# Cached grouped-query attention on one core: P·V two steps behind its scores, K three transfers ahead, last P·V by head group, held score weights

## The chip, the cores and the metric

One core of one Trainium2 chip runs the kernel. The metric is the device time of one execution in microseconds (us); lower is better. The profile is of one execution of the same program, taken by the hardware profiler.

## The reference

Each of 32 batches has 4 new tokens, 32 query heads and 4 key/value heads with a cache of 2048 positions. A query projection, attention over the whole cache, and an output projection are computed:

```python
B, Sq, D = 32, 4, 1024
Hq, Hkv, Sk, Dh = 32, 4, 2048, 128          # 8 query heads share a key/value head
q = (x @ wq).reshape(B, Sq, Hq, Dh).transpose(0, 2, 1, 3)
k = jnp.repeat(k_cache, 8, axis=1)
v = jnp.repeat(v_cache, 8, axis=1)
scores = einsum("bhqd,bhkd->bhqk", q, k) * Dh ** -0.5
o = einsum("bhqk,bhkd->bhqd", softmax(scores), v)
return o.transpose(0, 2, 1, 3).reshape(B, Sq, Hq * Dh) @ wo
```

All data are bfloat16. K and V of one batch are 2 MB each, so the caches alone are 128 MB; wq and wo are 8 MB each.

## The kernel before

Every operation is put into a list per engine by `p.op` or `p.dma`, in program order, with the names of the events that it waits for and the event that it sets. Each engine works its own list strictly in that order. An instruction that waits holds up everything behind it on its engine. "i" is the batch of a loop step and L = 31 the last batch.

**Loads.** All loads are issued by SP, in one list: x, the four parts of wq, then K and V by batch, one transfer of 2 MB each, and wo in four parts after V of batches 2 to 5. K and V have three buffers each (NKB = NVB = 3). `load_k(b)` (L133) waits until the last transposes of batch b−3 are done (`("fill", b-3, 7)`), `load_v(b)` (L142) until P·V of batch b−3 is done (`("pv", b-3)`). The order is K0, K1, then for each b: K(b+2), V(b). V of batch 31 is loaded in four pieces of 512 KB, one for each key/value head (L145). The twelve early output pieces follow on SP (L313).

**One loop step i** (the loop is near the end of the kernel) runs on TensorE in this order:

1. `pe_qk(i)` (L240): scores, 16 matmuls. Four column tiles of 32 hold 32 query rows (8 heads × 4 tokens) of one key/value head each; the loop goes over 4 chunks c of 512 positions and, inside, the 4 heads g. Each matmul has its own weight load. The result is in `ps_s` (128 × 2048 fp32[...]).
2. `pe_ot(i−2)` (L271): one transpose of the normalised o; ScalarE copies it to `oT_sb` (L275). After every eighth batch the output projection of that group of 8 batches follows (`oproj`, L296, 128 matmuls).
3. Two fills of batch i+1 (`pe_fill`, L207): K comes in natural layout, and TensorE transposes it, eight 128×128 blocks for each of eight fills. VectorE (L217) copies fills 2, 3, 5 and 7 to `KT_sb`, ScalarE (L219) the others.
4. The six other fills of batch i+1.
5. `pe_pv(i−1)` (L248): 64 matmuls (16 position blocks t × 4 heads g) with 32 columns of P^T as weights and V as moving operand.
6. `pe_pt(i, 0)`, `pe_pt(i, 1)` (L225): 16 transposes of P; VectorE copies each half to `PT_sb` (L231), which has one buffer, so the copy waits for P·V of batch i−1.

VectorE computes the row maximum (L280) and its scaled negative (L281), ScalarE the exponential with its row sum (L285), VectorE the reciprocal (L290). ScalarE normalises o after P·V (`o_evac`, L265). Fills, P^T, o, o^T and the projection's result rotate through a ring of four PSUM banks `ps_r`; a ring slot is free when the copy out of it is done.

**The end** is written out after the loop: o^T of batch 30, then P·V of batch 31 with heads 0 to 2 first and head 3 after them, two normalising copies on ScalarE (L357, L359), two transposes of o (L363, L371) with their copies (L364, L372), and the last output projection in two parts, heads 0 to 23 and 24 to 31 (L296 into `ps_s`). Then the last copy (L309) and four output transfers.

Of the kernel before, what the change touches and what calls it, by code (L numbers as in the profile page):

```python
# [5 lines left out]
ACT = mybir.ActivationFunctionType  # L6
ALU = mybir.AluOpType
AX = mybir.AxisListType
BF16 = mybir.dt.bfloat16
F32 = mybir.dt.float32  # L10


class _Program:
# [43 lines left out]
def bass_standalone__gqa_block_cached__sampling_kernel(  # L57
# [8 lines left out]
    B, Sq, D = x.shape  # L66
    _, G, Sk, Dh = k_cache.shape
    Hq = wq.shape[1] // Dh
    REP = Hq // G
# [6 lines left out]
    TV = T // C  # L76
    KT = D // 128
    NKB = 3
    NVB = 3
# [3 lines left out]
    OG = 8  # L83
    NOG = B // OG
    NC = D // 4
    scale = float(Dh) ** -0.5
# [5 lines left out]
    with ExitStack() as es:  # L92
        def sbuf(name, shape, dtype):
            return es.enter_context(nc.sbuf_tensor(name, shape, dtype))
# [6 lines left out]
        QT_sb = sbuf("QT_sb", [128, B, Hq, Sq], BF16)  # L101
        oT_sb = sbuf("oT_sb", [128, Hq, NT], BF16)
        P_sb = sbuf("P_sb", [128, Sk], BF16)
        PT_sb = sbuf("PT_sb", [128, TV, 128], BF16)
        x_sb = P_sb[:, 0:D]
        xT_sb = P_sb[:, D:2 * D].rearrange("p (a b) -> p a b", b=128)
        o_sb = sbuf("o_sb", [128, Dh], BF16)
# [15 lines left out]
        p = _Program()  # L123
# [8 lines left out]
        def load_k(b):  # L132
            p.dma("sp", lambda e: e.dma_start(  # L133
                K_sb[:, b % NKB, :, :], k_cache[b].rearrange("g (r t) d -> (g r) t d", r=R)),
                [("fill", b - NKB, NFILL - 1)] if b >= NKB else [], ("k", b), f"s_k{b % NKB}")
# [13 lines left out]
                wo_sb[:, 8 * c:8 * c + 8, :], wo[c * 1024:(c + 1) * 1024, :].rearrange("(h p) n -> p h n", p=128)),  # L149
                ["qproj"], ("wo", c), f"s_w{c}")  # L150

        load_k(0)
        load_k(1)
        for b in range(B):
            if b + 2 < B:
                load_k(b + 2)
            load_v(b)
            if b in (2, 3, 4, 5):
                load_wo(b - 2)
# [51 lines left out]
        def evac(b, f):  # L211
            buf = slot_of["kt", b, f]
            waits = [("fill", b, f)] + ([("qk", b - 1)] if b else [])
            dst = KT_sb[:, f * TB // C:(f + 1) * TB // C, :, :].rearrange("p v g (r c) -> p (v g) r c", c=C)
            src = buf.rearrange("p (c m r) -> p m r c", c=C, r=R)
            if f in DVE_FILLS:
                p.op("dve", lambda e: e.tensor_copy(dst, src), waits, ("kt", b, f))  # L217
            else:
                p.op("act", lambda e: e.activation(dst, src, ACT.Copy), waits, ("kt", b, f))  # L219

        def pe_pt(i, f):
            buf, waits = slot(("pt", i, f))
            buf = slot_of["pt", i, f] = buf.bitcast(BF16)
            for q in range(8):
                p.op("pe", lambda e, q=q: e.transpose(  # L225
                    buf[:, q * 128:(q + 1) * 128], P_sb[:, (8 * f + q) * 128:(8 * f + q + 1) * 128], ident[:, :]),
                    waits + [("exp", i)] if q == 0 else [], ("ptf", i, f) if q == 7 else None)

        def evac_pt(i, f):
            buf = slot_of["pt", i, f]  # L230
            p.op("dve", lambda e: e.tensor_copy(PT_sb[:, 8 * f:8 * f + 8, :].rearrange("p t q -> p (t q)"), buf),  # L231
                 [("ptf", i, f)] + ([("pv", i - 1)] if i else []), ("pt", i, f))


        def pe_qk(i):
            waits = [("kt", i, f) for f in range(NFILL)]
            waits += [("qe", j) for j in range(Hq // 4)] if i == 0 else [("exp", i - 1)]
            for c in range(4):
                for g in range(G):
                    p.op("pe", lambda e, c=c, g=g: e.matmul(  # L240
                        ps_s[32 * g:32 * (g + 1), c * 512:(c + 1) * 512],
                        lhsT=QT_sb[:, i, REP * g:REP * (g + 1), :],
                        rhs=KT_sb[:, 4 * c:4 * (c + 1), g, :],
                        start=True, stop=True, tile_position=(0, 32 * g)),
                        waits, ("qk", i) if (c, g) == (3, G - 1) else None)

        def pv_mm(buf, i, g, t, waits, done):
            p.op("pe", lambda e: e.matmul(  # L248
                buf[32 * g:32 * (g + 1), 0:Dh],
                lhsT=PT_sb[:, t, 32 * g:32 * (g + 1)],  # L250
                rhs=V_sb[:, i % NVB, g, t, :],
                start=(t == 0), stop=(t == TV - 1), tile_position=(0, 32 * g)), waits, done)
# [64 lines left out]
        for f in range(NFILL):  # L317
            pe_fill(0, f)
            evac(0, f)
        for i in range(B):  # L320
            pe_qk(i)
            softmax_max(i)
            if i >= 2:
                pe_ot(i - 2)
                ot_evac(i - 2)
                if i % OG == 1 and i > 1:
                    oproj(i // OG - 1)
            if i + 1 < B:
                for f in (0, 1):
                    pe_fill(i + 1, f)  # L330
                    evac(i + 1, f)
            softmax_exp(i)
            if i + 1 < B:
                for f in range(2, NFILL):
                    pe_fill(i + 1, f)
                    evac(i + 1, f)
            softmax_rinv(i)
            if i >= 1:
                pe_pv(i - 1)
                o_evac(i - 1)  # L340
            for f in range(2):
                pe_pt(i, f)
                evac_pt(i, f)


        L = B - 1
        pe_ot(L - 1)
        ot_evac(L - 1)
        o_l, waits = slot(None)
        waits = waits + [("pt", L, 0), ("pt", L, 1)]  # L350
        for t in range(TV):
            for g in range(3):
                pv_mm(o_l, L, g, t, waits + [("v", L, k) for k in range(3)] if t == 0 and g == 0 else [],
                      ("pva", L) if (t, g) == (TV - 1, 2) else None)
        for t in range(TV):
            pv_mm(o_l, L, 3, t, [("v", L, 3)] if t == 0 else [], ("pv", L) if t == TV - 1 else None)
        p.op("act", lambda e: e.activation(o_sb[0:96, :], o_l[0:96, 0:Dh], ACT.Copy, scale=rinv[0:96, L:L + 1]),  # L357
             [("pva", L), ("rinv", L), ("oT", L - 1)], "oa")
        p.op("act", lambda e: e.activation(o_sb[96:128, :], o_l[96:128, 0:Dh], ACT.Copy, scale=rinv[96:128, L:L + 1]),  # L359
             [("pv", L)], "ob")  # L360
        ta, waits = slot(None)
        ta = ta.bitcast(BF16)
        p.op("pe", lambda e: e.transpose(ta[:, 0:96], o_sb[0:96, :], ident[0:96, 0:96]), waits + ["oa"], "oTa")  # L363
        p.op("dve", lambda e: e.tensor_copy(  # L364
            oT_sb[:, 0:24, L * Sq:(L + 1) * Sq], ta[:, 0:96].rearrange("p (h s) -> p h s", s=Sq)), ["oTa"], "ota")
        y_l = ps_s[:, 0:512]
        n = NOG - 1
        oproj_mm(y_l, n, range(24), ["ota", ("ot", L - 1)], None)
        tb, waits = slot(None)
        tb = tb.bitcast(BF16)  # L370
        p.op("pe", lambda e: e.transpose(tb[:, 0:32], o_sb[96:128, :], ident[96:128, 96:128]), waits + ["ob"], "oTb")  # L371
        p.op("dve", lambda e: e.tensor_copy(  # L372
            oT_sb[:, 24:32, L * Sq:(L + 1) * Sq], tb[:, 0:32].rearrange("p (h s) -> p h s", s=Sq)), ["oTb"], "otb")
        oproj_mm(y_l, n, range(24, 32), ["otb"], ("op", n))
        oproj_evac(y_l, n)
        for m in range(NOG - 1):
            oproj_out(m, ("sp",))
# [57 lines left out]
```

## Time and profile before

| | before |
|---|---|
| device time, median of 9 runs | 387.11 us (385.98 to 387.68) |
| device time of the profiled execution | 387.25 us |
| its span on the core | 385.5 us |
| TensorE matmul busy | 281.7 us, 5929 matmuls |
| VectorE busy | 274.1 us |
| ScalarE busy | 208.4 us |
| moved by DMA | 152.32 MB, mean 395 GB/s over the span |
| mean granted TensorE clock | 0.946 |

The span is the time from the first to the last instruction on the core; 1.75 us of the profiled execution lie outside it. Busy time is the sum of the instructions of an engine; a share of it below 100% says nothing yet on what bounds the kernel. The chain of waits follows the work that ended last back through what released it. A DMA counts as landed when all its parts have landed.

### The profile page before, as it was taken

What the parts mean: (1) busy time and instruction counts of PE and PEld (TensorE: products, weight loads), DVE (VectorE), ACT (ScalarE), POOL (GpSimd) and SP (SyncE); (2) the same over time, 40 slices, a digit from 0 to 9 for tenths busy, and PEclk for the clock granted to TensorE, in tenths of its full rate; (3) what the DMA queues carried; (4) which work ended last, traced back from release to release, by engine and by line L of the source; (5) the groups of instructions that cost most, each with busy time, mean ns of one, the idle gap of its engine ahead of it and who ended that gap; (6) DMA issues with size and microseconds to landing.
All of it is one profiled execution on the core that took longest, in us unless ns stands there. A gap on an engine that the chain in (4) does not pass through costs nothing.

```text
span 385.5 us, 12595 instructions
## 1 busy us (share of the span) xinstructions
PE 281.7 (73%) x5929; PEld 230.8 (60%) x5929; DVE 274.1 (71%) x299; ACT 208.4 (54%) x261; POOL 0.7 (0%) x6
## 2 busy tenths in 40 slices
PE   2876888666383887887777778887759878876756
PEld 1875766556282766666655566665548666655545
DVE  0017999683553985998888849998868959997850
ACT  1005777355161646666666627766646566666620
POOL 0000000000000000000000000000000000000000
PEclk9999999896966999999999999999987999999978
DMA  8999999999999999999999999999999999999930
GB/s 328 432 432 414 420 418 396 414 407 399 411 408 414 415 420 412 417 415 419 417 416 419 417 413 420 416 414 417 413 417 416 420 416 418 419 417 409 375 140 9
DMA packets 27251, 152.32 MB, mean 395 GB/s; under 512 B 1472, under 2 KB 1984, under 8 KB 22592
## 3 DMA queue, kind: packets, MB, share of 16 engines
q1 hardware_dynamic: 27104, 151.49, 96.1%
q8 instruction: 46, 0.75, 0.8%
q10 hardware_dynamic: 96, 0.03, 0.0%
q14 instruction: 5, 0.04, 0.0%
HBM read 151.26 MB, written 0.26 MB: 393 GB/s over the span
## 4 chain that ended last, share of the span: by engine, by line
DMA 59%; PE 16%; ACT 12%; DVE 9%; issue 2%; SPq 1%
DMA K_sb<-in_k_cache_dram 59%; ACT KT_sb L219 6%; ACT P_sb L285 6%; DVE KT_sb L217 5%; PE ps_r L207 4%; PE ps_r L248 3%; DVE mx L280 3%; PE ps_r L296 3%; PE ps_r L225 3%; PE ps_s L240 2%; PE ps_s L296 1%; DVE PT_sb L231 0%; SPq L129 0%; ACT oT_sb L275 0%; DVE negmx L281 0%
## 5 line engine op out<-in xcount | busy, mean ns | idle before, releaser
L207 PE MATMUL ps_r<-ident,K_sb 128*128 128x128 bf16 x2048 | 143.3, 230 | 66.7 <-DMA K_sb<-in_k_cache_dram 41.5
L217 DVE COPY KT_sb<-ps_r 128x1024 bf16<-128x1024 bf16 x128 | 147.9, 1216 | 41.6 <-PE ps_r L207 41.5
L207 PEld LDWEIGHTS ps_r<-ident,K_sb 128*128 128x128 bf16 x2048 | 126.6, 104 | 82.3 <-DMA K_sb<-in_k_cache_dram 42.6
L219 ACT ACTIVATE KT_sb<-ps_r 128x1024 bf16<-128x1024 bf16 x128 | 124.4, 1026 | 72.1 <-PE ps_r L207 72.1
L280 DVE TENSOR_REDUCE mx<-ps_s 128x1 f32<-128x2048 f32 x32 | 73.3, 2292 | 6.7 <-PE ps_s L240 5.3
L285 ACT ACTIVATE P_sb<-ps_s,negmx 128x2048 bf16<-128x2048 f32 x32 | 63.0, 1970 | 2.2 <-DVE negmx L281 2.1
L231 DVE COPY PT_sb<-ps_r 128x1024 bf16<-128x1024 bf16 x64 | 41.4, 686 | 15.8 <-PE ps_r L225 14.2
L248 PE MATMUL ps_r<-V_sb,PT_sb 128*32 128x128 bf16 x2048 | 36.8, 223 | 16.6 <-ACT KT_sb L219 11.8
L248 PEld LDWEIGHTS ps_r<-V_sb,PT_sb 128*32 128x32 bf16 x2048 | 31.0, 98 | 22.1 <-ACT KT_sb L219 18.7
L275 ACT ACTIVATE oT_sb<-ps_r 128x128 bf16<-128x128 bf16 x31 | 8.6, 278 | 55.5 <-PE ps_r L271 55.5
L225 PE MATMUL ps_r<-ident,P_sb 128*128 128x128 bf16 x512 | 35.1, 223 | 1.7 <-ACT P_sb L285 1.3
L240 PE MATMUL ps_s<-KT_sb,QT_sb 128*32 128x512 bf16 x512 | 34.1, 382 | 2.3 <-DVE KT_sb L217 1.7
L225 PEld LDWEIGHTS ps_r<-ident,P_sb 128*128 128x128 bf16 x512 | 29.4, 99 | 5.3 <-ACT P_sb L285 1.5
L240 PEld LDWEIGHTS ps_s<-KT_sb,QT_sb 128*32 128x32 bf16 x512 | 10.8, 95 | 13.3 <-issue 2.8
L187 DVE CAST QT_sb<-ps_r 128x512 bf16<-128x512 f32 x2 | 1.3, 686 | 22.6 <-PE ps_r L176 22.6
L265 ACT ACTIVATE o_sb<-ps_r,rinv 128x128 bf16<-128x128 f32 x31 | 11.4, 367 | 9.8 <-PE ps_r L248 9.8
L189 ACT ACTIVATE QT_sb<-ps_r 128x512 bf16<-128x512 f32 x2 | 1.1, 594 | 26.1 <-PE ps_r L176 26.1
L176 PE MATMUL ps_s<-P_sb,w_sb 128*128 128x128 bf16 x128 | 9.7, 237 | 7.1 <-DMA w_sb<-in_wq_dram 7.1
L176 PEld LDWEIGHTS ps_s<-P_sb,w_sb 128*128 128x128 bf16 x128 | 8.6, 107 | 7.7 <-issue 4.4
L296 PE MATMUL ps_r<-w_sb,oT_sb 128*32 128x256 bf16 x384 | 11.3, 273 | 2.3 <-ACT oT_sb L275 1.2
L296 PEld LDWEIGHTS ps_r<-w_sb,oT_sb 128*32 128x32 bf16 x384 | 10.1, 97 | 3.2 <-issue 2.0
L271 PEld LDWEIGHTS ps_r<-ident,o_sb 128*128 128x128 bf16 x31 | 3.0, 98 | 12.7 <-issue 12.7
(30 smaller groups left out, 58.9 us busy)
## 6 DMA issues: line engine op xcount, KB each, us to landing
K_sb<-in_k_cache_dram SPq DMA_DIRECT2D x32, 2048.0 KB, 25.0
V_sb<-in_v_cache_dram SPq DMA_DIRECT2D x31, 2048.0 KB, 27.1
w_sb<-in_wq_dram SPq DMA_DIRECT2D x4, 2048.0 KB, 14.9
w_sb<-in_wo_dram SPq DMA_DIRECT2D x4, 2048.0 KB, 24.7
V_sb<-in_v_cache_dram SPq DMA_DIRECT2D x4, 512.0 KB, 15.5
P_sb<-in_x_dram SPq DMA_DIRECT2D x1, 256.0 KB, 2.7
out_dram<-y_sb SPq DMA_DIRECT2D x14, 16.0 KB, 11.5
out_dram<-y_sb ACTq DMA_DIRECT2D x2, 16.0 KB, 1.6
```

What stands on the lines that cost most here:

```text
L176: p.op("pe", lambda e, kt=kt, h=h: e.matmul(ps_q(h), lhsT=w_sb[:, kt, h * Dh:(h + 1) * Dh], rhs=xT_sb[:, kt, :], start=(kt == 0 and h % 4 ...
L207: p.op("pe", lambda e, q=q, t=t: e.transpose(buf[:, q * 128:(q + 1) * 128], K_sb[:, b % NKB, t, :], ident[:, :]), waits + [("k", b), "iden ...
L217: p.op("dve", lambda e: e.tensor_copy(dst, src), waits, ("kt", b, f))
L219: p.op("act", lambda e: e.activation(dst, src, ACT.Copy), waits, ("kt", b, f))
L225: p.op("pe", lambda e, q=q: e.transpose(buf[:, q * 128:(q + 1) * 128], P_sb[:, (8 * f + q) * 128:(8 * f + q + 1) * 128], ident[:, :]), wai ...
L231: p.op("dve", lambda e: e.tensor_copy(PT_sb[:, 8 * f:8 * f + 8, :].rearrange("p t q -> p (t q)"), buf), [("ptf", i, f)] + ([("pv", i - 1)] ...
L240: p.op("pe", lambda e, c=c, g=g: e.matmul(ps_s[32 * g:32 * (g + 1), c * 512:(c + 1) * 512], lhsT=QT_sb[:, i, REP * g:REP * (g + 1), :], rh ...
L248: p.op("pe", lambda e: e.matmul(buf[32 * g:32 * (g + 1), 0:Dh], lhsT=PT_sb[:, t, 32 * g:32 * (g + 1)], rhs=V_sb[:, i % NVB, g, t, :], star ...
L265: p.op("act", lambda e: e.activation(o_sb[:, :], buf[:, 0:Dh], ACT.Copy, scale=rinv[:, i:i + 1]), [("pv", i), ("rinv", i)] + ([("oT", i - ...
L280: p.op("dve", lambda e: e.tensor_reduce(mx[:, i:i + 1], ps_s[:, :], AX.X, ALU.max), [("qk", i)], ("mx", i))
L285: p.op("act", lambda e: e.activation(P_sb[:, :], ps_s[:, :], ACT.Exp, bias=negmx[:, i:i + 1], scale=scale, accum_out=ssum[:, i:i + 1]), [( ...
L296: p.op("pe", lambda e, h=h, j=j: e.matmul(buf[32 * j:32 * (j + 1), 0:NC], lhsT=oT_sb[:, h, 32 * n:32 * (n + 1)], rhs=wo_sb[:, h, NC * j:NC ...
```

## The change

It has five parts.

1. **P·V two steps behind.** Step i runs P·V of batch i−2 (was i−1) and o^T of batch i−3 (was i−2); the output projection of a group of 8 batches comes one step later. P·V of batch 30, o^T of 29 and of 30 move behind the loop.
2. **Load order.** K0, K1, K2, then for each b: K(b+3), V(b). Buffers and waits of each load stay as they were.
3. **Two P^T buffers.** `PT_sb` has two; a copy into it waits for P·V of batch i−2.
4. **The last P·V gives o^T.** P of batch 31 is normalised in place by one VectorE instruction over 128 × 2048 before its transposes. `pv_last(g)` has V (128 × 128) as weights and 32 columns of P^T as moving operand: 16 matmuls for each head group, after its own piece of V. One VectorE copy of 128 × 32 brings its o^T to `oT_sb`; `oproj_last(g)` does 32 matmuls of the output projection. TensorE's order is pv 0, pv 1, proj 0, pv 2, proj 1, pv 3, proj 2, proj 3. The ScalarE copies and TensorE transposes of the old end go.
5. **Held score weights.** Of the 16 score matmuls of a batch only those of the first chunk (c = 0) load weights; the 12 others are issued without a weight load and use what their column tile holds.

```diff
+def _matmul_held(nc, eng, out, lhsT, rhs, tile_position, start, stop):
+    return eng.add_instruction(mybir.InstMatmult(
...
+        tile_size=(128, 32),
+        tile_position=tile_position,
+        ldweights=False,
...
-        PT_sb = sbuf("PT_sb", [128, TV, 128], BF16)
+        PT_sb = sbuf("PT_sb", [128, 2, TV, 128], BF16)
...
-        load_k(0)
-        load_k(1)
+        for b in range(NKB):
+            load_k(b)
         for b in range(B):
-            if b + 2 < B:
-                load_k(b + 2)
+            if b + NKB < B:
+                load_k(b + NKB)
             load_v(b)
...
-                 [("ptf", i, f)] + ([("pv", i - 1)] if i else []), ("pt", i, f))
+                 [("ptf", i, f)] + ([("pv", i - 2)] if i > 1 else []), ("pt", i, f))
...
+                    if c == 0:
+                        mm = lambda e, a=(out, lhsT, rhs), g=g: e.matmul(
+                            a[0], lhsT=a[1], rhs=a[2], start=True, stop=True, tile_position=(0, 32 * g))
+                    else:
+                        mm = lambda e, a=(out, lhsT, rhs), g=g: _matmul_held(
+                            nc, e, *a, tile_position=(0, 32 * g), start=True, stop=True)
...
-            if i >= 2:
-                pe_ot(i - 2)
-                ot_evac(i - 2)
-                if i % OG == 1 and i > 1:
+            if i >= 3:
+                pe_ot(i - 3)
+                ot_evac(i - 3)
+                if i > OG and i % OG == 2:
                     oproj(i // OG - 1)
...
-            if i >= 1:
-                pe_pv(i - 1)
-                o_evac(i - 1)
+            if i >= 2:
+                pe_pv(i - 2)
+                o_evac(i - 2)
+            if i == L:
+                p.op("dve", lambda e: e.tensor_scalar(P_sb[:, :], P_sb[:, :], rinv[:, L:L + 1], None, op0=ALU.mult),
+                     [("rinv", L)], ("pn", L))
             for f in range(2):
-                pe_pt(i, f)
+                pe_pt(i, f, ("pn", L) if i == L else ("exp", i))
                 evac_pt(i, f)
...
+        pe_ot(L - 2)
+        ot_evac(L - 2)
+        pe_pv(L - 1)
+        o_evac(L - 1)
...
+        def pv_last(g):
+            buf, waits = slot(None)
+            for t in range(TV):
+                p.op("pe", lambda e, t=t: e.matmul(
+                    buf[:, 0:32], lhsT=V_sb[:, L % NVB, g, t, :], rhs=PT_sb[:, L % 2, t, 32 * g:32 * (g + 1)],
+                    start=(t == 0), stop=(t == TV - 1)),
+                    waits + [("v", L, g), ("pt", L, 0), ("pt", L, 1)] if t == 0 else [],
+                    ("pvl", g) if t == TV - 1 else None)
+            p.op("dve", lambda e: e.tensor_copy(
+                oT_sb[:, 8 * g:8 * (g + 1), L * Sq:(L + 1) * Sq], buf[:, 0:32].rearrange("p (h s) -> p h s", s=Sq)),
+                [("pvl", g)], ("otl", g))
+
+        def oproj_last(g):
+            oproj_mm(y_l, n, range(8 * g, 8 * (g + 1)), [("otl", g), ("ot", L - 1), ("exp", L)],
+                     ("op", n) if g == G - 1 else None)
+
         pe_ot(L - 1)
         ot_evac(L - 1)
-        o_l, waits = slot(None)
...
+        pv_last(0)
+        for g in range(G):
+            if g + 1 < G:
+                pv_last(g + 1)
+            oproj_last(g)
         oproj_evac(y_l, n)
```

More of the change, by code (lines that the diff above doesn't have):

```diff
@@ L10 @@
 F32 = mybir.dt.float32
+def _matmul_held(nc, eng, out, lhsT, rhs, tile_position, start, stop):
+    return eng.add_instruction(mybir.InstMatmult(
+        name=nc.get_next_instruction_name(),
+        engine=eng.engine,
+        start_tensor_calc=start,
+        stop_tensor_calc=stop,
+        tile_size=(128, 32),
+        tile_position=tile_position,
+        ldweights=False,
+        ins=[eng.lower_ap(rhs), eng.lower_ap(lhsT, for_matmul_weights=True)],
+        outs=[eng.lower_ap(out)],
+    ))
 class _Program:
@@ L219, in evac, with pe_pt @@
                 p.op("act", lambda e: e.activation(dst, src, ACT.Copy), waits, ("kt", b, f))
-        def pe_pt(i, f):
+        def pe_pt(i, f, ready):
             buf, waits = slot(("pt", i, f))
@@ L226, in pe_pt @@
                     buf[:, q * 128:(q + 1) * 128], P_sb[:, (8 * f + q) * 128:(8 * f + q + 1) * 128], ident[:, :]),
-                    waits + [("exp", i)] if q == 0 else [], ("ptf", i, f) if q == 7 else None)
+                    waits + [ready] if q == 0 else [], ("ptf", i, f) if q == 7 else None)
         def evac_pt(i, f):
             buf = slot_of["pt", i, f]
-            p.op("dve", lambda e: e.tensor_copy(PT_sb[:, 8 * f:8 * f + 8, :].rearrange("p t q -> p (t q)"), buf),
-                 [("ptf", i, f)] + ([("pv", i - 1)] if i else []), ("pt", i, f))
+            p.op("dve", lambda e: e.tensor_copy(PT_sb[:, i % 2, 8 * f:8 * f + 8, :].rearrange("p t q -> p (t q)"), buf),
+                 [("ptf", i, f)] + ([("pv", i - 2)] if i > 1 else []), ("pt", i, f))
         def pe_qk(i):
@@ L239, in pe_qk @@
                 for g in range(G):
[L240 to L245, printed above, removed]
+                    out = ps_s[32 * g:32 * (g + 1), c * 512:(c + 1) * 512]
+                    lhsT = QT_sb[:, i, REP * g:REP * (g + 1), :]
+                    rhs = KT_sb[:, 4 * c:4 * (c + 1), g, :]
+                    if c == 0:
[4 more added lines that the diff above has]
+                            nc, e, *a, tile_position=(0, 32 * g), start=True, stop=True)
+                    p.op("pe", mm, waits, ("qk", i) if (c, g) == (3, G - 1) else None)
         def pv_mm(buf, i, g, t, waits, done):
@@ L249, in pv_mm @@
                 buf[32 * g:32 * (g + 1), 0:Dh],
-                lhsT=PT_sb[:, t, 32 * g:32 * (g + 1)],
+                lhsT=PT_sb[:, i % 2, t, 32 * g:32 * (g + 1)],
                 rhs=V_sb[:, i % NVB, g, t, :],
@@ L319, in bass_standalone__gqa_block_cached__sampling_kernel @@
             evac(0, f)
+        L = B - 1
         for i in range(B):
@@ L322, in bass_standalone__gqa_block_cached__sampling_kernel @@
             softmax_max(i)
-            if i >= 2:
-                pe_ot(i - 2)
-                ot_evac(i - 2)
-                if i % OG == 1 and i > 1:
+            if i >= 3:
+                pe_ot(i - 3)
+                ot_evac(i - 3)
+                if i > OG and i % OG == 2:
                     oproj(i // OG - 1)
-            if i + 1 < B:
+            if i < L:
                 for f in (0, 1):
@@ L332, in bass_standalone__gqa_block_cached__sampling_kernel @@
             softmax_exp(i)
-            if i + 1 < B:
+            if i < L:
                 for f in range(2, NFILL):
@@ L343, in bass_standalone__gqa_block_cached__sampling_kernel @@
                 evac_pt(i, f)
-        L = B - 1
+        pe_ot(L - 2)
+        ot_evac(L - 2)
+        pe_pv(L - 1)
+        o_evac(L - 1)
+        y_l = ps_s[:, 0:512]
+        n = NOG - 1
+        def pv_last(g):
[9 more added lines that the diff above has]
+                [("pvl", g)], ("otl", g))
@@ L347, in bass_standalone__gqa_block_cached__sampling_kernel @@
+        def oproj_last(g):
+            oproj_mm(y_l, n, range(8 * g, 8 * (g + 1)), [("otl", g), ("ot", L - 1), ("exp", L)],
+                     ("op", n) if g == G - 1 else None)
         pe_ot(L - 1)
         ot_evac(L - 1)
-        o_l, waits = slot(None)
[L350 to L371, printed above, removed]
@@ L372, in bass_standalone__gqa_block_cached__sampling_kernel @@
-        p.op("dve", lambda e: e.tensor_copy(
-            oT_sb[:, 24:32, L * Sq:(L + 1) * Sq], tb[:, 0:32].rearrange("p (h s) -> p h s", s=Sq)), ["oTb"], "otb")
-        oproj_mm(y_l, n, range(24, 32), ["otb"], ("op", n))
+        pv_last(0)
[3 more added lines that the diff above has]
+            oproj_last(g)
         oproj_evac(y_l, n)
```

## The prediction

> **What bounds the kernel now.** I read the page's slices first, then its queues, then stages of the last 25 us, and last the chain and the timeline there.
>
> ```profile
> DMA  8999999999999999999999999999999999999930
> q1 hardware_dynamic: 27104, 151.49, 96.1%
> q8 instruction: 46, 0.75, 0.8%
> ```
>
> Tenths of DMA busy time in 40 slices, then packets, MB and share of two queues. From the second slice to the 37th the DMA engines are full, and nearly all of it is SP's own loads. No engine in that stretch sets the time: a step costs 8.65 us where the compute runs ahead (o^T transposes at 54.27, 62.92 and 71.56 in the timeline), but 4 MB of K and V take 10.0 us (K transfers released their transposes at 348.60 and 358.58). The slack is 1.4 us a step. So only a later start, a hole in the queue, a step above 10 us or the end can move the time.
>
> ```profile
> 362.00:364.00 2.00, 0.92 (x14) 0.58 (x11) 2.00 (x3) 2.00 (x4) 0.00 (x0) 1.00 1.02 403
> 364.00:366.00 2.00, 1.90 (x80) 1.80 (x80) 1.06 (x3) 1.33 (x3) 0.00 (x0) 1.00 0.72 274
> 370.00:372.00 2.00, 0.52 (x13) 0.35 (x14) 0.16 (x1) 2.00 (x3) 0.00 (x0) 0.87 0.55 202
> 372.00:374.00 2.00, 1.82 (x17) 1.56 (x15) 0.94 (x2) 0.17 (x2) 0.00 (x0) 0.50 0.22 72
> 374.00:376.00 2.00, 1.50 (x48) 1.50 (x52) 0.45 (x1) 0.14 (x1) 0.00 (x0) 0.50 0.00 0
> ```
>
> Columns: stretch, its length, busy time of PE, PEld, DVE, ACT and POOL with counts, clock, DMA share, GB/s. Half of the DMA engines are done near 365, the last ones near 374. The last piece of V31 (issued at 358.1, 15.5 us to landing) lands at 373.6, the first (355.2, 14.6) at 369.8. After it come 12 us without loads. Below are links of the chain in order of time (start, us, what), then two lines of the timeline.
>
> ```profile
> 358.54 0.05 issue
> ...
> 367.20 2.30 DVE mx L280
> ...
> 369.72 2.07 ACT P_sb L285 x2
> ...
> 371.83 1.90 PE ps_r L225 x16
> ...
> 374.50 3.16 PE ps_r L248 x61
> ...
> 378.15 2.85 PE ps_s L296 x72
> ```
> ```profile
> 368.75 0.94 PE L248 MATMUL ps_r<-V_sb,PT_sb 128*32 128x128 bf16 x53 [1.43 <-DMA V_sb<-in_v_cache_dram]
> 382.50 0.42 DVE L309 CAST y_sb<-ps_s 128x256 bf16<-128x256 f32 x1 [1.17 <-PE ps_s L296]
> ```
>
> The chain starts at K31's landing (358.54): its transposes, scores, maximum, exponential, P^T, P·V and projection end at 382.92, and output and end take 2.6 us more. P·V of 31 begins at 374.50, just after V31 is complete: both paths meet there.
>
> [...] clock 0.50 from about 371.5, after a quiet stretch, though not a fully idle one.
>
> **The change, part by part.** DMA volume and work per step are the same.
>
> *Load order.* K31 now has V28 to V31 behind it, where it had V29 to V31: it lands one transfer of 5.0 us earlier, at 353.6. V28 takes its place (358.5), V29, V30 and V31 keep theirs, since the same bytes pass the same engines. The queue's depth in mid-run stays: before, SP passed K(i+4), V(i+2) after fills and P·V of step i; now K(i+4), V(i+1), each needed one step later. At the start V0 now stands behind K3, which waits for the fills of batch 0 (34.4). Until then 3.4 + 4.2 + 4.4 + 1.9 = 13.8 MB have moved (336, 424, 436 and 430 GB/s); x, wq and K0 to K2 are 14.9 MB, 2.6 us more. The first load, x, took 2.7 us from issue to landing: no hole, at most 0.3 us. At the end V31 waits for P·V of 28, which now runs after the fills of K31 and V28's landing, near 359.2 to 360.3 (355.2 before). Its four issues took 4.1 us, so the fast engines, through with V30 at about 359, idle some 3 to 4 us; the slow ones, which set the end, reach V31 only at 368.6. Cost 0; behind V31 on SP stand only the outputs of finished groups.
>
> *P·V delay, two P^T buffers.* 64 P·V matmuls, a copy and a transpose per step move, none is added. P·V(i−2) meets V where P·V(i−1) did: one transfer behind the K filled just before. The P^T copy's wait gets looser. All lies under the loads: 0.
>
> *Held weights.* 32 × 12 = 384 loads of 95 ns (L240) go, overlapped with matmuls of 382 ns; a block of scores still streams for 1.05 us, so 0. The q8 row fetches 16 KB packets, so at most two fewer; each delays one DMA engine by about 1 us: 0 to −1.7 us, I take 0.
>
> *The end*, in the profile's time. K31 at 353.6. Scores of 31 started 7.5 us after K31's landing and ended 8.6 after: 362.2. P·V 29 runs at 363.7 (V29) for 1.1. Maximum, scaling and exponential end 13.2 after the landing: 366.8. Reciprocal 0.15; the normalisation is not in the trace. Nearest rows: P^T copy 686 ns for 1024 (PSUM source), so 1.3 for 2048; the maximum's 2.3 is a ceiling.[...] P^T starts at 367.8.
>
> From here TensorE is the path, and its clock decides. From 362.4 to 367.8 it does only 1.1 us of work, as little as ahead of the 0.50 stretch before. So I expect half speed from about 367 until[...] 371.8 to 374.8; middle 373.4. At half speed: 16 transposes 1.9 (to 369.7), o^T 29 0.3, P·V 30 from 370.1, 2 × 1.08 to 372.25 (V30 is there at 368.6), its copy 0.4, o^T 30, and the first pv_last at 372.75.
>
> Then pv_last: 64 matmuls with 128-column weights. The row L225 has such weight loads at 0.90/16 = 56 ns with more moving columns: 0.9 per group.[...] I take 56[...]. Projection: 128 × 28.8 ns (3.68 us at L296) = 3.68. Sum 3.6 + 3.68 = 7.28; its copies (0.17, as L372, plus 0.3 of waits) lie under the next 0.9 block, and pieces of V31 are ahead of it. Half speed until 373.4 adds 0.33: 380.35; latency 0.2, last copy 0.44: 381.0 against 382.92, **−1.9 us**. Removed with the old end: copies L357 and L359, two transposes, and the split P·V's 3.16 at half speed; they are inside this comparison.
>
> The profiled execution would then be 387.25 − 1.9 = 385.35; it lies 0.14 above the median, so 387.11 − 1.9 = **385.2**.
>
> **Rivals.** Chances in brackets.
>
> 1. *Forecast: faster, end bound by TensorE at partly half clock* (0.50). Clock back at 371.8 gives −2.5, at 374.8 −1.2: 384.6 to 385.9; with pv_last at 40 ns another −1.0.
> 2. *Faster, clock full at the end[...]* (0.27). At full clock P^T takes 1.0, P·V 30 starts at 369.0, pv_last at 370.5; +7.28, +0.64: 378.45, −4.5, 382.6.[...] Against it: the gap from 362.4. The bound from V31 (373.64 + 0.5 + 1.84 + 0.64 = 376.6) is −6.3.
> 3. *The gain is given back* (0.11). Half clock until 378.3, as before: 5.55 us at half lose 2.78: 372.75 + 7.28 + 2.78 + 0.64 = 383.45, +0.5; with partial recovery about 0. Against it: pv and projection leave no gap of the kind that stood at 373.7 and 376.4.
> 4. *Slower: held weights break the overlap of the four column tiles* (0.07). Then 16 score matmuls of 512 columns run in turn: 16 × 213 ns (the 1.05 us block, less 0.2 of latency, is 4 such rounds) = 3.4, +2.35 per step against 1.4 of slack: +0.95 × 30 = +28 us, 415. It decides from a block above 2.5 us. For it: no row shows a matmul without its load. Against: tiles, positions and streaming stay.
> 5. *The late normalisation or the order of loads costs more than it saves* (0.05): VectorE at 2.3 rather than 0.7 with half clock to 376 adds 1.6 + 0.6: +0.3; with a start hole of 1 us, 388.4.
>
> If the held form reloaded weights anyway, nothing changes in time.
>
> **How the numbers follow.** A difference of 0.2%, 0.8 us, is what a measurement here can tell from none. Cases 1 and 2 are faster (0.77, plus 0.01 of 3); 3 is mostly the same (0.10); 4 and 5 slower (0.12). The likeliest is 385.2. The range 382.3 to 387.4 holds case 1, case 2 nearly to the end of its full-clock form, and case 3.
>
> **What would show it.** K31's transposes start near 353.6; SP issues V31 near 360; V31's last piece still near 373.6; TensorE busy without a gap from about 368; a normalisation of about 0.7 us; pv_last groups of 0.9 us; score blocks of 1.05 us with 4 weight loads; the last copy ending near 381. Wrong if the last loads land more than 1 us from 373.6, if score blocks grow, or if the clock stays full after 367.

## The result, and the profile after

The changed kernel took 383.11 us (median of 10 runs, 382.3 to 383.94), the kernel before 386.89 us (32 runs, 384.83 to 387.68). The ratio is 0.9907, with a 95% interval of 0.9893 to 0.9922: 3.6 us faster. Measured a second time it was 0.9905 (0.9886 to 0.9924). The forecast was 1.9 us. The direction and the mechanism were right; the size forecast was little more than half of what came.

The page of the kernel after, slices of DMA busy time and two queues:

```profile
DMA  8999999999999999999999999999999999999870
q1 hardware_dynamic: 27104, 151.49, 97.1%
q8 instruction: 45, 0.74, 0.8%
```

The loads are as full as before, now in a span of 382.0 us instead of 385.5. Two stages of the kernel after (columns as in the prediction):

```profile
370.00:372.00 2.00, 2.00 (x59) 1.80 (x61) 1.21 (x2) 0.28 (x1) 0.00 (x0) 0.50 0.56 210
374.00:376.00 2.00, 2.00 (x73) 1.70 (x72) 0.38 (x2) 0.00 (x0) 0.00 (x0) 1.00 0.03 9
```

The loads still end near 374 (the DMA records have V31's last piece at 373.9). What differs is TensorE: it works in every moment of both stages, where before it had 0.52 us of work between 370 and 372. K31 has landed a transfer earlier; its transposes, which began at 358.58 before, begin at 352.36:

```profile
352.36 2.41 PE L223 MATMUL ps_r<-ident,K_sb 128*128 128x128 bf16 x40 [1.24 <-DMA K_sb<-in_k_cache_dram]
```

The chain of waits of the kernel after, near the end (start, us, what):

```profile
358.49 1.84 PE ps_r L268 x64
...
363.16 2.30 DVE mx L300
...
365.68 2.07 ACT P_sb L305 x2
...
367.96 0.77 DVE P_sb L363
...
368.78 1.86 PE ps_r L241 x16
...
370.75 1.77 PE ps_r L268 x63
...
373.27 0.86 PE ps_r L380 x32
374.13 0.99 PE ps_s L316 x32
...
377.10 1.89 PE ps_s L316 x64
...
379.01 0.42 DVE y_sb L329
```

It starts at V28 now, not at K31: P·V of 28 at 358.49, then maximum, exponential, normalisation (L363), P^T, P·V of 30, the new P·V (L380) and the projection (L316), which end at 379.43 instead of 382.92. The 3.49 us between these two are the whole difference of the spans.

This profiled execution took 383.77 us. Another one of the same kernel (after_again, 382.44 us) differs from it at two places that matter below, the first P·V of this stage and the end:

```profile
358.51 1.08 PE L268 MATMUL ps_r<-V_sb,PT_sb 128*32 128x128 bf16 x64 [1.20 <-DMA V_sb<-in_v_cache_dram]
...
377.58 0.42 DVE L329 CAST y_sb<-ps_s 128x256 bf16<-128x256 f32 x1 [1.68 <-PE ps_s L316]
```

P·V of 28 starts at the same time but takes 1.08 us instead of 1.84, because the half clock lies elsewhere (365.1 to 371.9), and the end comes 1.43 us earlier. Single traces must be compared with this in mind; the ratios are over all executions.

### The profile page after: what moved, and what is told of

The parts are those of the page before. It is cut to its first block, busy times and chain, and to the rows that moved or that the text cites. A ratio compares the mean times of both kernels' runs of the same rounds, so it can differ in the third digit from the quotient of the medians.

```text
span 382.0 us, 12207 instructions
## 1 busy us (share of the span) xinstructions
PE 278.8 (73%) x5927; PEld 220.3 (58%) x5543; DVE 274.7 (72%) x302; ACT 207.4 (54%) x259; POOL 0.7 (0%) x6
## 4 chain that ended last, share of the span: by engine, by line
DMA 60%; PE 16%; ACT 11%; DVE 10%; issue 2%; SPq 1%
DMA K_sb<-in_k_cache_dram 53%; DMA V_sb<-in_v_cache_dram 7%; ACT KT_sb L235 6%; ACT P_sb L305 5%; DVE KT_sb L233 5%; PE ps_r L223 4%; DVE mx L300 4%; PE ps_r L316 3%; PE ps_r L268 3%; PE ps_r L241 3%; PE ps_s L16 1%; PE ps_s L316 1%; PE ps_s L260 1%; DVE PT_sb L247 1%; PE ps_r L380 0%
## 5 line engine op out<-in xcount | busy, mean ns | idle before, releaser
L223 PE MATMUL ps_r<-ident,K_sb 128*128 128x128 bf16 x2048 | 138.2, 225 | 61.8 <-DMA K_sb<-in_k_cache_dram 36.8
L223 PEld LDWEIGHTS ps_r<-ident,K_sb 128*128 128x128 bf16 x2048 | 120.9, 101 | 79.7 <-DMA K_sb<-in_k_cache_dram 37.9
L268 PE MATMUL ps_r<-V_sb,PT_sb 128*32 128x128 bf16 x1984 | 35.8, 228 | 17.6 <-ACT KT_sb L235 12.6
L268 PEld LDWEIGHTS ps_r<-V_sb,PT_sb 128*32 128x32 bf16 x1984 | 30.1, 101 | 22.9 <-ACT KT_sb L235 22.0
L241 PE MATMUL ps_r<-ident,P_sb 128*128 128x128 bf16 x512 | 36.6, 228 | 4.3 <-DVE P_sb L363 4.0
L241 PEld LDWEIGHTS ps_r<-ident,P_sb 128*128 128x128 bf16 x512 | 30.8, 102 | 8.0 <-DVE P_sb L363 4.2
L16 PE MATMUL ps_s<-KT_sb,QT_sb 128*32 128x512 bf16 x384 | 26.3, 379 | 0.0
L260 PE MATMUL ps_s<-KT_sb,QT_sb 128*32 128x512 bf16 x128 | 12.8, 389 | 2.8 <-DVE KT_sb L233 1.7
L316 PE MATMUL ps_r<-w_sb,oT_sb 128*32 128x256 bf16 x384 | 11.5, 273 | 3.1 <-issue 1.9
L316 PEld LDWEIGHTS ps_r<-w_sb,oT_sb 128*32 128x32 bf16 x384 | 10.1, 97 | 4.0 <-issue 2.9
```

Source lines behind the costliest of these rows:

```text
L16: return eng.add_instruction(mybir.InstMatmult(name=nc.get_next_instruction_name(), engine=eng.engine, start_tensor_calc=start, stop_tenso ...
L223: p.op("pe", lambda e, q=q, t=t: e.transpose(buf[:, q * 128:(q + 1) * 128], K_sb[:, b % NKB, t, :], ident[:, :]), waits + [("k", b), "iden ...
L241: p.op("pe", lambda e, q=q: e.transpose(buf[:, q * 128:(q + 1) * 128], P_sb[:, (8 * f + q) * 128:(8 * f + q + 1) * 128], ident[:, :]), wai ...
L260: mm = lambda e, a=(out, lhsT, rhs), g=g: e.matmul(a[0], lhsT=a[1], rhs=a[2], start=True, stop=True, tile_position=(0, 32 * g))
L268: p.op("pe", lambda e: e.matmul(buf[32 * g:32 * (g + 1), 0:Dh], lhsT=PT_sb[:, i % 2, t, 32 * g:32 * (g + 1)], rhs=V_sb[:, i % NVB, g, t, : ...
L316: p.op("pe", lambda e, h=h, j=j: e.matmul(buf[32 * j:32 * (j + 1), 0:NC], lhsT=oT_sb[:, h, 32 * n:32 * (n + 1)], rhs=wo_sb[:, h, NC * j:NC ...
```

## The experiments

Differences in microseconds are ratios to the kernel before, times 387. Every kernel ran beside the kernel before on the same chip. Theory A is the prediction's mechanism with one price corrected. Its rivals are B (the new end alone is the gain), C (the held weights give a part) and, later, D (late instructions decide).

### The price of the new P·V

```diff
-                    buf[:, 0:32], lhsT=V_sb[:, L % NVB, g, t, :], rhs=PT_sb[:, L % 2, t, 32 * g:32 * (g + 1)],
+                    buf[:, 0:128], lhsT=V_sb[:, L % NVB, g, t, :], rhs=PT_sb[:, L % 2, t, :],
...
```

> The changed kernel, but the 64 matmuls of pv_last stream all 128 columns of P^T instead of 32 (the other 96 result columns are not used). Theory A: TensorE sets the end without a gap from P·V of batch 30 on, and the forecast missed by the price of one pv_last matmul (29 ns in the profile after, 56 in the sum). Then 64 x (56 - 29) = 1.7 us come back: 384.8 us, 1.9 below before, and pv_last groups of 0.9 us. Rival: V31's landing or something else sets the end and the price is hidden: 383.1, as the changed kernel.

384.64 us, ratio 0.9945 (0.9930 to 0.9959): 1.5 us slower than the changed kernel, 2.1 faster than before. One group each of the timelines of the kernel after and of wide_pv:

```profile
375.05 0.57 PE L380 MATMUL ps_r<-PT_sb,V_sb 128*128 128x32 bf16 x16
```
```profile
374.00 1.07 PE L380 MATMUL ps_r<-PT_sb,V_sb 128*128 128x128 bf16 x16
```

Both have the same weights and the same waits. With the moving operand as wide as the one from which I took 56 ns, a group takes 1.07 us, and the gain is back near the forecast. With 32 columns it takes 0.57; the chain has 0.50 for a group, 31 ns a matmul. So the price was wrong and it lies on the path: theory A. The two profiled executions themselves took the same time (383.82 and 383.77 us), since that of wide_pv lacks the half clock ahead of the scores; but from the first pv_last to the end of the projection it needed 7.78 us (371.14 to 378.92) against 5.78 (373.18 to 378.96).

### Which parts carry the gain

Each of these five undoes one part or does one part alone.

*The old end with everything else changed.*

```diff
...
-        pv_last(0)
-        for g in range(G):
-            if g + 1 < G:
-                pv_last(g + 1)
-            oproj_last(g)
+        o_l, waits = slot(None)
+        waits = waits + [("pt", L, 0), ("pt", L, 1)]
+        for t in range(TV):
+            for g in range(3):
...
```

> The changed kernel with the end of before: o = P·V for batch 31 in two parts, normalising copies on ScalarE, transposes, projection in two parts; no normalisation of P. Load order, P·V delay, two P^T buffers and held weights stay. Theory A: the gain comes from K31 landing a transfer earlier, and the new end is worth little, since it pays for the normalisation of P and its 1.0 us: about +0.7 on the changed kernel, 383.8. Theory B: the shorter work after V31 is the gain: 386 or more.

385.74 us, ratio 0.9977 (0.9965 to 0.9988): 0.9 us of the gain is left. Neither theory's number came. Timeline of old_end:

```profile
372.77 3.16 PE L268 MATMUL ps_r<-V_sb,PT_sb 128*32 128x128 bf16 x64 [2.44 <-DMA V_sb<-in_v_cache_dram]
376.42 3.37 PE L316 MATMUL ps_s<-w_sb,oT_sb 128*32 128x256 bf16 x96 [0.30 <-DVE oT_sb L388]
```

P^T is ready at 368.3, so the earlier K31 has done its part. But the old end asks for three pieces of V31 at once and idles for 2.44 us; then its P·V and the first 1.2 us of its projection run in a half-clock stretch (370.8 to 377.6). I had expected only +0.7 us on the changed kernel; it is +2.7.

*The new end alone, on the kernel before.*

```diff
...
+            if i == B - 1:
+                p.op("dve", lambda e: e.tensor_scalar(P_sb[:, :], P_sb[:, :], rinv[:, B - 1:B], None, op0=ALU.mult),
+                     [("rinv", B - 1)], ("pn", B - 1))
...
+        pv_last(0)
+        for g in range(G):
+            if g + 1 < G:
+                pv_last(g + 1)
+            oproj_last(g)
```

> The kernel before with only the new end (normalised P, pv_last by head group, projection by head group); load order, P·V one step behind and all weight loads stay. K31 lands at 358.5 as before, so P^T is ready near 375.3, 0.9 later than before because of the normalisation; then 1.9 + 3.7 us of TensorE work, part of it at half clock, against 8.4 us of the old end. Theory A (the two parts need each other): about 0.5 us below before, 386.3, far from the whole gain. Theory B (the new end alone is the gain): 383.5.

387.68 us, ratio 1.0021 (1.0011 to 1.0031): 0.8 us slower than before. Theory B falls, and the 0.5 us of gain that theory A expected did not come either. Timeline of new_end_only:

```profile
376.38 1.02 PE L356 MATMUL ps_r<-PT_sb,V_sb 128*128 128x32 bf16 x32 [0.77 <-DVE PT_sb L231]
377.32 1.90 PE L296 MATMUL ps_s<-w_sb,oT_sb 128*32 128x256 bf16 x32
```

P^T is ready only at 376.2, when V31 is complete (374.4): there is no landing left to work under, the normalisation is added, and projection blocks run at half speed. In this execution the loads also landed 0.8 us later than in the profile before, K31 at 359.34 instead of 358.54. It is the slowest of its 22 (386.98 to 388.59), so what the landings have to do with the +0.8 of the medians is not shown.

*The load order of before, all else changed.*

```diff
-        for b in range(NKB):
-            load_k(b)
+        load_k(0)
+        load_k(1)
...
-            if b + NKB < B:
-                load_k(b + NKB)
+            if b + 2 < B:
+                load_k(b + 2)
```

> The changed kernel with the load order of before (K0, K1, then K(b+2), V(b)); all else stays changed. Theory A: K31 lands a transfer (5.0 us) later, its exponential ends at 371.8 as before, normalisation, P^T, P·V 30 and the new end follow: about 4 us above the changed kernel, 387.2, no better than before. Theory B (the new end is the gain, the order of loads is not): 383 to 384.

387.90 us, ratio 1.0028 (1.0014 to 1.0042): 4.7 us above the changed kernel, 0.7 more than expected. Timeline of k_two_ahead:

```profile
373.18 1.89 PE L241 MATMUL ps_r<-ident,P_sb 128*128 128x128 bf16 x16 [3.68 <-DVE P_sb L363]
```

P^T of 31 starts at 373.18, in the kernel after at 368.78 (at 367.22 in after_again): 4.4 to 6.0 us, around the one transfer of 5.0. This kernel and new_end_only differ only in P·V's delay, the P^T buffers and the held weights; their ratios, 1.0028 and 1.0021, do not differ beyond their intervals. Without the new load order these three gained nothing.

*The load order alone, on the kernel before.*

```diff
-        load_k(0)
-        load_k(1)
+        for b in range(NKB):
+            load_k(b)
...
-            if b + 2 < B:
-                load_k(b + 2)
+            if b + NKB < B:
+                load_k(b + NKB)
```

> The kernel before with only the load order changed (K three ahead of V); P·V stays one step behind, one P^T buffer, old end, all weight loads. Theory A: P·V of batch i-1 now waits for a V that lands 15 us after the K of batch i+1 instead of 5, and it stands on TensorE ahead of the scores of the next batch. So P·V 28 starts at V28's landing (358.5), the transposes of K31 only near 361.5 though K31 is there at 353.6, and the exponential of 31 ends near 374.5 instead of 371.8: slower, about 389.5. Rival: the load order alone gives the gain: 383.5.

391.52 us, ratio 1.0120 (1.0102 to 1.0138): 4.6 us slower than before, where 2.6 were expected. Timeline of order_only:

```profile
358.41 1.08 PE L248 MATMUL ps_r<-V_sb,PT_sb 128*32 128x128 bf16 x64 [2.60 <-DMA V_sb<-in_v_cache_dram]
...
362.78 2.64 PE L207 MATMUL ps_r<-ident,K_sb 128*128 128x128 bf16 x40
...
375.64 0.35 PE L248 MATMUL ps_r<-V_sb,PT_sb 128*32 128x128 bf16 x11 [3.02 <-issue]
...
376.25 1.31 PE L225 MATMUL ps_r<-ident,P_sb 128*128 128x128 bf16 x16 [0.27 <-ACT P_sb L285]
```

P·V of 28 waits for V28, and the transposes of K31 start at 362.78, though K31 had landed at 353.15. That is the mechanism named. Part of the other 2 us is half clock (359.9 to 363.3), which the expectation did not have: P^T of 29 and the scores of 30, behind P·V of 28, ran slower, the transposes of K31 began 1.3 us later than the 361.5 expected, and the exponential ended at 376.20 instead of 374.5. The profiled execution is also the fastest of the four (390.60 to 392.12); the rest was not traced. In P·V of 30 TensorE then waited 3.02 us for nothing visible, of which more below. It cost nothing here: that P·V was done at 375.99, and P^T of 31 waited for the exponential anyway (last line).

*Held weights undone.*

```diff
-                    if c == 0:
-                        mm = lambda e, a=(out, lhsT, rhs), g=g: e.matmul(
-                            a[0], lhsT=a[1], rhs=a[2], start=True, stop=True, tile_position=(0, 32 * g))
-                    else:
-                        mm = lambda e, a=(out, lhsT, rhs), g=g: _matmul_held(
-                            nc, e, *a, tile_position=(0, 32 * g), start=True, stop=True)
+                    mm = lambda e, a=(out, lhsT, rhs), g=g: e.matmul(
+                        a[0], lhsT=a[1], rhs=a[2], start=True, stop=True, tile_position=(0, 32 * g))
```

> The changed kernel with a weight load for each of the 16 score matmuls again (held weights undone). Theory A: the loads lie under 512-column matmuls and the score block stays at 1.05 us; only 384 more instructions are fetched: within 0.3 us of the changed kernel. Rival C: the held weights gave a part of the gain, through shorter score blocks or through fewer instruction packets on the DMA engines: 0.8 us or more above the changed kernel.

 

> The changed kernel once more, beside the other kernels of this call on the same chip: 0.9907 of before as first measured, about 383.2 us. It is the base of the next differences. No theory differs on it.

383.05 us beside 383.46 of the changed kernel, measured together; ratios 0.9904 (0.9887 to 0.9920) and 0.9905. The score block, in the timelines of no_held and of the kernel after:

```profile
361.04 1.05 PE L259 MATMUL ps_s<-KT_sb,QT_sb 128*32 128x512 bf16 x16
```
```profile
362.08 0.40 PE L260 MATMUL ps_s<-KT_sb,QT_sb 128*32 128x512 bf16 x4
362.30 0.82 PE L16 MATMUL ps_s<-KT_sb,QT_sb 128*32 128x512 bf16 x12
```

From 362.08 to 363.12 it is 1.04 us, with 4 loads or with 16. Rival C falls, as far as a difference of 0.8 us can be seen here, and so does the prediction's fourth rival: the four column tiles still overlap, since 16 matmuls of 379 to 389 ns each fit into 1.04 us.

### The clock at the end, and a second limit

With the price settled I asked whether the half-clock stretches of the end (358.6 to 362.0 and 368.84 to 372.25 in the kernel after) could be taken away, by idle work on TensorE in its gaps: 24 transposes of the identity ahead of P·V of 28, and 44 behind P·V of 29, ahead of the P^T transposes.

```diff
...
+            if i == L - 1:
+                keep_warm("a", 24)
...
             if i == L:
+                keep_warm("b", 44)
```

> The changed kernel plus 24 idle transposes of the identity on TensorE ahead of P·V 28 and 44 ahead of the P^T transposes of batch 31, into a ring slot that nobody reads, to keep the clock granted. Theory A (the end is TensorE work, a part of it at half clock): in the profile after, half speed cost 0.8 us on P·V 28, 0.8 on P^T 30 and, later, 0.8 on P^T 31 and 0.7 on P·V 30; without it about 2 us less, 381.2, with V31's last landing (373.9 + 3.0) as the new bound. Rival: the clock is not on the path, or the idle transposes stand in the way: 383.1 or more.

384.05 us, ratio 0.9928 (0.9911 to 0.9945): 0.9 us slower than the changed kernel. The clock was full from 356.6 to the end, P^T took 1.07 us, and still the end came later. Timeline of warm:

```profile
365.89 0.68 PE L268 MATMUL ps_r<-V_sb,PT_sb 128*32 128x128 bf16 x34 [1.35 <-issue]
...
369.48 1.07 PE L241 MATMUL ps_r<-ident,P_sb 128*128 128x128 bf16 x16 [0.34 <-DVE P_sb L374]
...
371.90 0.63 PE L268 MATMUL ps_r<-V_sb,PT_sb 128*32 128x128 bf16 x32 [0.74 <-issue]
...
377.10 0.72 PE L324 MATMUL ps_s<-w_sb,oT_sb 128*32 128x256 bf16 x18 [0.90 <-issue]
```

In the middle of a block TensorE stops three times for nothing visible, 3.0 us in all. The first stop was over before the normalised P came, so about 1.6 us of it lay on the path; and P^T began at 369.48, 0.7 us later than in the kernel after, since the fillers ahead of P·V of 28 had pushed the scores back to 362.77. The DMA records of the instruction queue (q8) have a packet of 16 KB that ends at 364.44, 370.60 and 375.49, which is 1.3 to 1.6 us ahead of each resumption. This holds for the long stops of the other traces too: in the kernel before, the stops that end at 148.65, 229.42 and 310.99 follow packets that end at 147.12, 228.02 and 309.51. In the 16 traces there are 58 waits of TensorE for "issue" above 0.6 us, and 57 of them end 1.2 to 1.6 us after a packet; the one of order_only above ends 2.25 us after. So I read "issue" inside a block as late instructions (theory D). So the fillers were made longer and fewer, 6 and 11 matmuls of 512 columns in the same two places (warm_long; shown against warm):

```diff
...
-                p.op("pe", lambda e, q=q: e.transpose(
-                    buf[:, (q % 8) * 128:(q % 8 + 1) * 128], ident[:, :], ident[:, :]),
+                p.op("pe", lambda e: e.matmul(
+                    buf[:, 0:512], lhsT=ident[:, :], rhs=wo_sb[:, 0, 0:512], start=True, stop=True),
...
```

> As warm, with the same TensorE time filled by 6 and 11 matmuls of 512 columns instead of 24 and 44 transposes of 128: 102 fewer instructions, counting weight loads. In warm the clock was full to the end and yet 3.0 us of waits for nothing the profile shows stood on TensorE (1.35 in P·V 29, 0.74 in P·V 30, 0.9 in the projection). Theory D: those are late instructions[...]; then the long form has under 1 us of such waits and comes to 382 or less. Rival: the added TensorE work itself is in the way; then as warm, 384.1.

382.45 us, ratio 0.9891 (0.9875 to 0.9906), and no stop above 0.6 us after 240. About the same busy time (4.0 against 4.1 us) with fewer instructions is 1.4 us faster than warm. Against the changed kernel it is 0.6 us, inside the intervals. In warm_few 6 of them stand ahead of P·V of 29 and 8 behind it, none ahead of P·V of 28; few_split also normalises P in two halves.

```diff
...
             if i == L:
+                keep_warm("b", 6)
             if i >= 2:
                 pe_pv(i - 2)
                 o_evac(i - 2)
             if i == L:
+                keep_warm("c", 8)
...
```
```diff
...
+                for f in range(2):
+                    half = P_sb[:, 1024 * f:1024 * (f + 1)]
+                    p.op("dve", lambda e, half=half: e.tensor_scalar(half, half, rinv[:, L:L + 1], None, op0=ALU.mult),
+                         [("rinv", L)], ("pn", f))
...
```

> The changed kernel plus 14 matmuls of 512 columns on TensorE, 6 ahead of P·V 29 and 8 behind it, where it waits for V29 and for the normalised P. Theory A (half clock at the end costs): P^T of 31 at 1.07 instead of 1.86 us and P·V 30 at 1.08 instead of 1.81, so 1 to 1.5 us below the changed kernel, about 382.0. Rival: the clock is worth nothing, because V30 and V31 land late enough to hide it: 383.2.

 

> As warm_few, with the normalisation of P in two halves, each followed by its own transposes. Half of 0.75 us comes off the path: 0.3 us below warm_few, about 381.7. If V30's landing (368.5) holds up P·V 30 anyway: as warm_few.

Both came out at 386.7 us, ratios 0.9997 (0.9978 to 1.0015) and 0.9989 (0.9966 to 1.0011): 3.3 to 3.6 us worse than the changed kernel, against both theories in their text. few_split's timeline shows how:

```profile
370.38 0.89 PE L392 MATMUL ps_r<-PT_sb,V_sb 128*128 128x32 bf16 x19
374.64 0.51 PE L392 MATMUL ps_r<-PT_sb,V_sb 128*128 128x32 bf16 x13 [3.37 <-issue]
```

TensorE stops after the third matmul of the second group. The packet that began at 368.15 in the kernel after and at 368.29 in the profile of warm_few began at 372.22 here, and half clock came with the stop (371.7 to 378.5). The lateness is not the same in every execution: of the 14 executions of warm_few the traced one took 382.32 us and has no such stop, while the other 13 took 386.07 to 387.91; one of few_split's 14 took 382.05. If late packets are the cause, moving the packet boundaries must move the time, and one must ask whether the measured change owes its size to such a boundary. So 24 idle transposes (48 instructions) were put near 4.6 us, where TensorE waits for wq:

```diff
+        for q in range(24):
+            p.op("pe", lambda e, q=q: e.transpose(
+                ring[3].bitcast(BF16)[:, (q % 8) * 128:(q % 8 + 1) * 128], ident[:, :], ident[:, :]))
```

> warm_few with the same 24 idle transposes near 4.6 us. The unprofiled runs of warm_few lay near 386.7, its profiled one at 382.3, and few_split's profile has a 3.4 us wait for nothing visible in pv_last, which ends 1.5 us after an instruction packet. Rival D (late instructions): the padding moves the boundary and the time changes by 2 us or more, to about 382.5. If the added 512-column matmuls themselves cost the 4 us: still 386.7.

 

> The changed kernel plus 24 idle transposes of the identity on TensorE near 4.6 us, while it waits for the first part of wq: 48 more instructions ahead of all others, 2.6 us of work under the wait. Theory A (the gain comes from K31's earlier landing and the new end): 383.2, as the changed kernel. Rival D (where the packets[...] begin decides whether TensorE runs dry at the end, and the changed kernel has a lucky place): up to 4 us more, 386 to 387.

 

> The kernel before with the same 24 idle transposes near 4.6 us. Theory A: 386.9, as before. Rival D: the place of the instruction packets costs the kernel before something that the padding changes: off by more than 1 us, to either side.

| kernel | without padding | with padding |
|---|---|---|
| before | 1 | 1.0001 (0.9987 to 1.0016) |
| changed | 0.9905 (0.9886 to 0.9924) | 0.9896 (0.9881 to 0.9910) |
| warm_few | 0.9997 (0.9978 to 1.0015) | 0.9903 (0.9886 to 0.9920) |

The padding takes 3.6 us away from warm_few and nothing from the two kernels compared here. So the 3.6 us of warm_few hang on where its instructions begin, and the change's gain does not hang on it, as far as this one shift shows. That the 3.6 us are a late packet is shown only for few_split, a near relative, by its trace; for warm_few it is inferred, since no execution near 386.7 us was traced. Why a packet comes late in some executions and not in others stays open. Full clock at the end, without the stops, was worth no more than the 0.6 us of warm_long here; few_pad, whose half-clock stretch only moved to an earlier place (359.4 to 362.8), is level with the changed kernel. No version is shown to be better than it.

## Why the prediction was right in kind and short in size

- **Loads set the pace and do not move.** Right. V31's last piece at 373.9 against 373.6; no hole at the start; SP issued V31 at 360.36, as forecast near 360, and it cost nothing.
- **K31 one transfer earlier.** Right: its transposes began at 352.36, 1.2 us ahead of the 353.6 of the sum. That was spent again: a half-clock stretch from 358.6 to 362.0, not forecast, stretched P·V of 28 and P^T of 30 to 1.8 us each, and the scores of 31 began at 362.08 against 361.1. In after_again, without that stretch, they began at 360.52.
- **Exponential and normalisation.** The exponential ended at 367.75 against 366.8; the normalisation took 0.75 us. The sum counts 0.7 for it, a number that the trace of before did not show; the nearest row there gave 1.3.
- **Half clock from about 367 until about 373.4.** Right in kind, and over P^T and P·V of 30 as forecast, but it came later and ended earlier: 368.84 to 372.25 (365.1 to 371.9 in after_again). Its end, 371.8 to 374.8 in the forecast, was my estimate: the trace of before did not show what ends such a stretch. First pv_last at 373.15 against 372.75. That this came out so close is partly luck: in after_again it was 371.70.
- **The step that failed: pv_last's price.** 64 × 56 ns = 3.6 us was the term; the chain has 0.86 + 0.50 + 0.50 = 1.86. These 1.7 us are all of the gap between 381.0 and 379.43 and more. The row that I took streams 128 columns, and its 56 ns were not a limit of its weight load: with such loads and 32 columns 27 to 31 ns were measured in the chain. The 1.5 us between wide_pv and the changed kernel are this term, turned on and off.
- **Old end against new end.** The sum compared two absolute ends and never priced the old end under the new load order. old_end shows that it would have lost 2.7 us; the load order and the delay without the new end bring 0.9, the new end without them −0.8, all together 3.6. The forecast was right to cost them as one path.
- **Nothing for held weights, P^T buffers, P·V's delay in mid-run.** For the held weights no_held shows it. P·V's delay and the two P^T buffers were not tried alone, but with the old load order the three together gained nothing (k_two_ahead beside new_end_only). With the new order they are worth 5.5 us: old_end (0.9977) and order_only (1.0120) differ in just these three. So the delay costs nothing and is what lets the new order gain.

## What to carry to other kernels

When loads bound a kernel, look at what stands between the landing of the last operand and the end: reorder the loads so that the long chain's operand comes first, move the work that waits for the other operand out of that chain's way, and cut the work on the last operand by its pieces. Here the new order alone lost 4.6 us, with P·V delayed it gained 0.9, the new end alone lost 0.8, and all together gained 3.6. Price a small matmul by its own moving width: 16 with the same weights took 0.57 us with 32 moving columns and 1.07 with 128, so here the wider row only bounded it from above. And a few microseconds at the end can be instructions that come late (3.37 us in few_split); more instructions near the end can make that worse (3.0 us of stops in warm), and a shift of where they begin can take it away (3.6 us, few_pad against warm_few).

## What the runs showed of the hardware

- A 128-column weight load with 32 moving columns went at about 30 ns a matmul at full clock (0.95 us for 32 in the kernel after), and hardly slower at half: 1.02 us for 32 in new_end_only, where the clock was 0.50. With 128 moving columns it was 1.07 us for 16 at full clock (wide_pv), and 16 transposes took 1.89 at half (the kernel before, from 371.83) against 1.07 at full (warm).
- Half clock came also after stretches in which TensorE worked, not only after idle ones (0.00 us of work from 84.75 in the kernel before). Cut the trace of the kernel before, from 13.07 us on, where its clock record begins, into pieces of 3.41 us, the length of its shortest half-clock stretch: pieces at full clock with up to 1.59 us of TensorE work were followed by half clock, and pieces with 1.61 or more were not (records of matmuls may be missing in either). This line is no threshold for the other kernels: in the kernel after, pieces with 1.62 us (355.19 to 358.60) and 1.65 (293.75 to 297.16) were followed by half clock, and one with 1.51 (20.68 to 24.09) was not.
- In the traces of the kernel before and the kernel after, every half-clock stretch that ended within the trace lasted 3.41 us (358.60 to 362.01 in the kernel after), or twice that (371.47 to 378.30 in the kernel before) or three times (123.08 to 133.32 in the kernel after). Where it began near the end differed between the two executions of the changed kernel (358.60 and 368.84; 365.10), and the end with it, by 1.4 us.
- Instructions come in packets of 16 KB (queue q8), which the profile counts on the same 16 DMA engines: 45 in the kernel after, 46 in the kernel before with its 386 weight loads more, about 1.07 us each. An estimate from the kernel before, if q8 holds TensorE's alone: 11,858 matmuls and weight loads in 46 packets are some 258 to a packet. After 57 of the 58 long waits for "issue" TensorE resumed 1.2 to 1.6 us behind a packet, and the longest at the end was 3.37 us (few_split). That each packet delays the loads by its 1.07 us, as the prediction counted, was not tried.
- The DMA engines do not end together: in the kernel after V31's last piece had landed on the first of them at 367.55 and on the last at 373.91. Whether the instruction packets cause that lag was not tried.
